# Own buffers and three move queues for the last two chunks, longer-counted stores, idle products up to the end

## The chip, the cores and the metric

The kernel runs on one core of one Trainium2 chip. The metric is the device time of one execution in microseconds; the median of the runs is given. Profiles are of one execution, with times from the first instruction of the span. Five engines work side by side, each in its own order: TensorE (PE; PEld is its weight loads), VectorE (DVE), ScalarE (ACT), GpSimd (POOL) and SyncE (SP); SP, ACT and POOL also issue DMAs.

## What is computed

A linear recurrence with a state per head, and behind it a gated projection with a causal convolution. All is float32; `B, H, S, D = 4, 8, 768, 40`.

```python
state = zeros(B, H, D, D)
for t in range(S):
    y[t]  = r[t] @ state                       # per head
    Sa    = state @ a[t]
    state = state * w[t] - outer(Sa, b[t]) + outer(v[t], k[t])

x = y as [B, S, 320]
gate = sigmoid(sum(conv_w[k] * x shifted by 4 - k  for k in range(5)))
out  = (gate * (x @ w_val)) @ w_out
```

## The kernel before

Time is cut into 12 chunks of 64 steps. For each chunk a preparation (`prep`, L458) makes cumulative decays with two scans on VectorE and scales the inputs; `tri` (L528) inverts triangular 32x32 blocks for two chunks at once in many small steps on VectorE; `solve` (L562) builds the 64x64 inverses on TensorE; `chain` (L614) is the recurrence itself. A chain works in two halves `hf` (8 of 16 head pairs each) through products `u0`, `u`, `t`, `g`, `ys`, each followed by an eviction on ACT or VectorE. Its last eviction `ye` (L680) writes the chunk's output x into `XE[c % 2]`.

Behind the chain stands the gated projection:

- `moves(c)` (L735) rearranges x for the projection by DMAs from `xe` to `xt`: 8 for the first half of the heads, 4 for the second (L742). For chunks 0 to 9 they go on POOL, for the last two, which `single` (L732) picks out, on SP.
- `moe(c)` (L746) runs once for each pair of chunks 0 to 9 (after the odd one), and once for each of chunks 10 and 11. Its steps, with names: `cv` (the convolution: one step of three pieces on ACT, L755, then four steps of three pieces on VectorE, L759), `gate` (sigmoid on ACT, L763), `val` (x @ w_val on TensorE, L89, in two parts), `gm` (gate times value on VectorE, L765 and L768), `out` (the product with w_out, L112), `os` (its eviction on ACT, L773), `store` (DMA to HBM, L780; on ACT, for chunk 11 every second one on SP). `val` and `out` use one pair of PSUM banks, PM, so they take turns with `gm` and `os`.
- `room(c)` (L724) says where this lies. Pairs use all of `XTW` (tile `xt`) for the input and `AG` (tile `ag`) for convolution, gate and product; the stored result is written over the convolution. Chunks 10 and 11 use a half each of the same two tiles, and so wait for the pair before them by the keys `XK`, `AK`, `GK`.

The order of the work is planned before the kernel is built. `Plan.op` (L155) registers each step with its engine, a duration in ns, what it reads and writes, and `lat`, the time from its end until another engine may use its result. `Plan.order` (L176) runs a greedy list scheduler with 80 random starts and 5 refinements each over all steps of the whole kernel, walks each order through a model of the engines, and keeps the one with the shortest modelled time. Each engine then executes its steps in exactly that order. Where the model sees TensorE waiting for over 0.48 us, `greedy` (L198) puts in idle products on a constant (L221 to L229, emitted at L832), which keep TensorE occupied; each goes to a PSUM bank that is free at that time.

`KB` (tile `kb`) is a ring of two tiles with the inputs k and b of a chunk; `prep`, `ak` (L494) and `turn` (L508) read it. The last of the 12 chunks' readers are done some 60 us before the last chunk's chain begins to write its output. `ind` is a constant operand of the scans; column C of it is overwritten by each chunk's `rc` (L469) and reset by `ic` (L473).

Of the kernel before, what the change touches and what calls it, by code (L numbers as in the profile page):

```python
# [147 lines left out]
class Plan:  # L148
# [27 lines left out]
    def order(self, fill):  # L176
# [21 lines left out]
        def greedy(rank, before, after, gap, tensor=None, weight=0, slack=0):  # L198
# [9 lines left out]
            for _ in range(N):  # L208
# [12 lines left out]
                if pe and end[cst]:  # L221
                    x = max(free["PE"], end[cst] + 3000)
                    while x + WARM + 150 < t:
                        k = next((k for k in banks if last[k] + 1 < len(users[k]) and eng[users[k][last[k] + 1]] == "PE" and
                                  (last[k] < 0 or eng[users[k][last[k]]] != "PE" and end[users[k][last[k]]] + 300 < x)), None)
                        if k is None:
                            break
                        more.append((x, -1 - banks.index(k)))
                        x = tensor.run(x, WARM, 4, 384)  # L229
# [103 lines left out]
def fast_path(ctx, tc, ins, out, nch, cst, wts, wz, wmx, fl):  # L333
# [37 lines left out]
    XE = ring("xe", 2, [128, P16, C + 4])  # L371
    XTW = new("xt", [128, 2 * 680])
    AG = new("ag", [128, 40 * C])
# [84 lines left out]
    def prep(c):  # L458
# [6 lines left out]
        def flat(x):  # L465
# [6 lines left out]
           r=wk + [("wpad", int(c == 1)), "ind"], w=["y0"])  # L472
        op(("ic", c), "DVE", 60, lambda: V.memset(ind[:, :, C:C + 1], WLO ** C), w=["ind"])  # L473
        op(("far", c), "ACT", act(1024) + 140, lambda: A.activation(out=wv, in_=wv, func=AF.Abs, bias=bias[:, 0:1]), r=["bias"], w=wk)
# [225 lines left out]
    def weigh():  # L700
# [3 lines left out]
        for i in range(NWT // WB):  # L704
            f = (XTW if i % 2 else AG)[:, 0:4 * WB].bitcast(I32)
            keys = XK if i % 2 else AK + GK[0:2]

            def wload(i=i, f=f):
                st_[i] = convert_ops(nc, f, wts[:, i * WB:(i + 1) * WB])
                dma(f[:, 0:2 * WB], src[:, 2 * i * WB:2 * (i + 1) * WB])  # L710
            op(("wd", i), "SP", 870, wload, w=keys, lat=2500)
            for j in range(8):
                op(("wc", i, j), "DVE", WCD[j], lambda i=i, j=j: st_[i][j](), w=keys + ["wts"])
# [7 lines left out]
    wv, wo, cw = weights(wts, wz)  # L721
    XK, AK, GK = [("xt", 0), ("xt", 1)], [("acc", 0), ("acc", 1)], [("gv", 0), ("gv", 1), "n1"]

    def room(c):  # L724

        i, L = c % 2, C if single(c) else 2 * C
        h = i if single(c) else 0
        xt = XTW[:, h * 680:h * 680 + 10 * (L + 4)].rearrange("p (b t) -> p b t", b=10)
        acc, gf = [AG[:, o + h * 640:o + h * 640 + 10 * L] for o in (0, 20 * C)]
        return (L, xt, acc, gf) + ((XK[i:i + 1], AK[i:i + 1], GK[i:i + 1]) if single(c) else (XK, AK, GK))  # L730

    def single(c):  # L732
        return c + 2 >= nch

    def moves(c):  # L735
# [3 lines left out]
        for hf in range(2):  # L739
            def xd(hf=hf):  # L740
                for o, x in x_moves(xt, XE[i], C, hf, lo, at):
                    (nc.sync if single(c) else G).dma_start(out=o, in_=x)  # L742
            op(("xd", c, hf), "SP" if single(c) else "POOL", (8, 4)[hf] * (400 if single(c) else 600), xd,
               r=[("xe", i, hf)] + ([] if lo else [("xe", i, "c")]) + ["wts"], w=xk, lat=2500)

    def moe(c):  # L746
# [5 lines left out]
        nn = [4 * L, 4 * L, 2 * L]  # L752
        part = [[("cv", x, k) for x in ((c % 2,) if single(c) else (0, 1))] for k in range(3)]
        for k, q in enumerate(qs):
# [19 lines left out]
        for b in range(B):  # L774
# [3 lines left out]
            else:  # L778
                to, of = out[b, c * C - C:c * C + C], accf[:, b * DM:b * DM + DM]
            op(("store", c, b), on, 560, lambda to=to, of=of, eng=eng: eng.dma_start(out=to, in_=of), r=ak, lat=2000)  # L780

# [187 lines left out]
```

## Time and profile before

| | before |
|---|---|
| median of 3 runs | 457.69 us (457.06 to 459.44) |
| profiled execution: its time / its span | 458.0 us / 456.2 us |
| mean granted TensorE clock | 0.961 of full |
| busy: TensorE / VectorE / ACT / POOL | 407.6 / 351.0 / 216.8 / 81.4 us |
| moved by DMA | 63.15 MB |

Busy time of TensorE contains the idle products, and its matmuls are pipelined, so a busy TensorE is not one at its peak. The granted clock is a share of full speed (2.4 GHz); half is 1.2 GHz.

### The profile page before, as it was taken

The numbers are of one execution on the slowest core, as the hardware profiler recorded it, in microseconds if no ns is written. First come the engines' busy times: TensorE is split into PE (matmuls) and PEld (weight loads), VectorE is DVE, ScalarE is ACT, GpSimd is POOL, SyncE is SP. The second block draws the span as 40 slices with busy tenths as digits, with TensorE's granted clock in tenths as the row PEclk, the third lists the DMA queues.
The fourth block names the chain that finished last, engine by engine and source line by source line (L and its number), as shares of the span: only waits on it lengthen the run. The fifth ranks groups of instructions, "written<-read, shape, count | busy, mean of one in ns | idle before, by whom it ended". The sixth has DMA issues, their size and how long they took to land.

```text
span 456.2 us, 19899 instructions
## 1 busy us (share of the span) xinstructions
PE 407.6 (89%) x9007; PEld 346.5 (76%) x9007; DVE 351.0 (77%) x673; ACT 216.8 (48%) x368; POOL 81.4 (18%) x169
## 2 busy tenths in 40 slices
PE   0799989899999899989999599989999999999773
PEld 0798868888988688888877588877797787778551
DVE  8999968999988959889899389949898950823530
ACT  1963466364962452973706490804772355333110
POOL 2010000236000515000461000007600533000000
PEclk9999999999999999999999799979999999999956
DMA  8897320575605525624665304533304235002111
GB/s 330 337 356 251 101 105 4 178 244 189 222 4 170 188 73 191 225 57 164 225 207 153 136 5 168 208 123 116 90 4 168 57 120 178 3 18 74 31 30 34
DMA packets 19689, 63.15 MB, mean 138 GB/s; under 512 B 4576, under 2 KB 8944, under 8 KB 16528
## 3 DMA queue, kind: packets, MB, share of 16 engines
q1 hardware_dynamic: 12400, 54.64, 34.4%
q0 software_dynamic: 3840, 3.42, 3.0%
q10 hardware_dynamic: 3360, 3.77, 2.5%
q8 instruction: 72, 1.18, 1.1%
q14 instruction: 17, 0.14, 0.1%
HBM read 53.77 MB, written 3.93 MB: 126 GB/s over the span
## 4 chain that ended last, share of the span: by engine, by line
PE 77%; ACT 7%; issue 4%; DMA 3%; SPq 2%; DVE 1%; ACTq 0%; DVEq 0%
PE pc L653 9%; PE pm L89 9%; PE pc L667 8%; PE pm L112 8%; PE pp L502 5%; PE pm L832 5%; PE pp L514 4%; PE pc L643 4%; PE pc L669 4%; PE pc L627 3%; DMA out<-ag 3%; PE pc L636 3%; PE pc L625 2%; PE pp L484 2%; PE pc L832 2%
## 5 line engine op out<-in xcount | busy, mean ns | idle before, releaser
L742 POOL DMA_DIRECT2D xt<-xe x120 | 73.8, 622 | 193.7 <-PE pm L89 100.4
L759 DVE SCALAR_TENSOR_TENSOR ag<-xt,wts,ag 128x512 f32<-128x512 f32 (+2 forms) x84 | 47.4, 590 | 13.5 <-ACT ag L755 9.7
L655 DVE TENSOR_TENSOR mu<-pc,cst 128x1024 f32<-128x1024 f32 x24 | 29.3, 1222 | 35.9 <-PE pc L653 28.1
L554 DVE TENSOR_TENSOR tm<-x 128x58 f32<-128x58 f32 (+9 forms) x164 | 51.9, 317 | 2.8
L556 DVE TENSOR_TENSOR x<-x,tm 128x58 f32<-128x58 f32 (+9 forms) x164 | 52.0, 317 | 2.3
L653 PE MATMUL pc<-ra,vu 64*128 64x64 f32 x768 | 47.2, 277 | 3.1 <-issue 2.8
L653 PEld LDWEIGHTS pc<-ra,vu 64*128 64x128 f32 x768 | 45.0, 191 | 4.6 <-issue 2.9
L832 PE MATMUL pm<-cst 128*128 128x192 f32 x218 | 42.5, 343 | 2.1 <-ACT tt L590 1.6
L667 PE MATMUL pc<-mu,kbt 128*64 128x104 f32 x768 | 40.7, 261 | 0.0
L112 PE MATMUL pm<-wts,ag 128*128 128x320 f32 (+1 forms) x144 | 39.8, 473 | 0.8 <-DVE ag L768 0.8
L832 PEld LDWEIGHTS pm<-cst 128*128 128x128 f32 x218 | 36.3, 196 | 3.7 <-ACT tt L590 2.1
L667 PEld LDWEIGHTS pc<-mu,kbt 128*64 128x64 f32 x768 | 36.0, 140 | 3.1 <-issue 0.2
L89 PE MATMUL pm<-xt,wts 128*128 128x256 f32 (+3 forms) x168 | 33.4, 383 | 4.6 <-ACT ag L773 2.9
L112 PEld LDWEIGHTS pm<-wts,ag 128*128 128x128 f32 (+1 forms) x144 | 22.0, 196 | 14.0 <-issue 6.9
L516 ACT COPY kbt<-pp 128x640 f32<-128x640 f32 x24 | 16.6, 693 | 32.1 <-PE pp L514 16.8
L89 PEld LDWEIGHTS pm<-xt,wts 128*128 128x128 f32 (+1 forms) x168 | 23.4, 189 | 10.9 <-ACT ag L773 3.4
L478 DVE TENSOR_TENSOR kb<-kb,y 104x1024 f32<-104x1024 f32 x24 | 29.0, 1212 | 1.0 <-DMA kb<-in_kb 0.9
L484 PE MATMUL pp<-at,kb 64*64 64x64 f32 x768 | 15.5, 234 | 16.0 <-DVE kb L478 13.3
L688 ACT COPY zd<-pc 104x320 f32<-104x320 f32 x22 | 9.1, 428 | 42.7 <-PE pc L685 25.4
L484 PEld LDWEIGHTS pp<-at,kb 64*64 64x64 f32 x768 | 13.7, 146 | 18.5 <-DVE kb L478 13.6
L502 PE MATMUL pp<-at,kb 64*64 64x64 f32 x768 | 25.5, 220 | 1.6 <-issue 1.1
L502 PEld LDWEIGHTS pp<-at,kb 64*64 64x64 f32 x768 | 23.6, 135 | 4.1 <-issue 1.7
(110 smaller groups left out, 757.6 us busy)
## 6 DMA issues: line engine op xcount, KB each, us to landing
kb<-in_kb SPq DMA_DIRECT2D x12, 1024.0 KB
vu<-in_vt SPq DMA_DIRECT2D x12, 1024.0 KB
ra<-in_ra SPq DMA_DIRECT2D x12, 832.0 KB
at<-in_a SPq DMA_DIRECT2D x12, 512.0 KB
w<-in_w SPq DMA_DIRECT2D x11, 520.0 KB
vp<-in_vp SPq DMA_DIRECT2D x12, 320.0 KB
out<-ag ACTq DMA_DIRECT2D x20, 160.0 KB
xt<-xe POOLq DMA_DIRECT2D x30, 42.5 KB, 3.7
```

The costliest lines, as they stand in the source:

```text
L89: T.matmul(out=o, lhsT=wv[k][r, m * 128:min(m * 128 + 128, DM)], rhs=rhs, start=(k == 0), stop=(k == 2))
L112: nc.tensor.matmul(out=ps[:, j, 0:DM], lhsT=gv[r, q:q + 128], rhs=wo[k][r], start=(k == 0), stop=(k == 2))
L484: T.matmul(out=PP[rows(par ^ s, 64), s, q * C:q * C + C], lhsT=KB[kb][rk, 2 * q + s, 1], rhs=at[rk, 2 * q + s], start=True, stop=True)
L502: T.matmul(out=PP[r, s, q * C:q * C + C], lhsT=KB[kb][r, 2 * q + s, 0], rhs=AT[n][r, 2 * q + s], start=True, stop=True)
L554: V.tensor_tensor(out=tv, in0=part(32 * (j + 1) + j, *b, (32, n), (0, j)), in1=part(32 * j, *b, (0, n), (1, j)), op=ALU.mult)
L556: V.tensor_tensor(out=x, in0=x, in1=tv, op=ALU.subtract)
L653: T.matmul(out=ps[:, s, i * C:i * C + C], lhsT=vu[r, 8 * hf + i].rearrange("p b t -> p (b t)"), rhs=ra[r, w, 0:C], start=True, stop=True)
L655: op(("ge", c, hf), "DVE", dve(1024), lambda: V.tensor_tensor(out=mu[:, :, 0:C].rearrange("p (i s) t -> p s i t", s=2), in0=ps.rearrange(" ...
L667: T.matmul(out=o, lhsT=KBT[k][:, y * D:y * D + C], rhs=mu[:, 2 * (4 * p + q4) + s], start=(not c and not q4), stop=(q4 == 3))
L742: (nc.sync if single(c) else G).dma_start(out=o, in_=x)
L759: op(("cv", c, j, k), "DVE", 130 + 1.04 * nn[k], lambda k=k, q=q, j=j: V.scalar_tensor_tensor(out=acc[:, q], in0=xt[:, q, j:j + L], scalar ...
L832: return lambda: T.matmul(out=bank[:, 1, 0:192], lhsT=ident, rhs=cst[:, 0:192], start=True, stop=True)
```

## The change

1. Idle products may also go to a bank that has no user left, not only to one whose next user is TensorE.
2. `XTW` shrinks to what a pair needs. Chunks 10 and 11 take input, convolution and product from `KB[0]` and `KB[1]`, with keys of their own; the keys of pairs become single names.
3. `moves`: a table of queues with a planned cost for each issue (SP 750, POOL 550, ACT 600 ns), and `split`, which deals out the DMAs of each half: for pairs all on POOL as before (planned at 550 instead of 600 ns), for chunk 10 on SP (4 and 2) and POOL (4 and 2), for chunk 11 on SP (3 and 1), POOL (3 and 2) and ACT (2 and 1). Each share is a step of its own in the plan.
4. The latency that the plan counts for a store is 6000 instead of 2000 ns.
5. The reset `ic` of `ind` becomes a copy on ACT from the column beside it, instead of a memset on VectorE.

```diff
-                        k = next((k for k in banks if last[k] + 1 < len(users[k]) and eng[users[k][last[k] + 1]] == "PE" and
+                        k = next((k for k in banks if (last[k] + 1 == len(users[k]) or eng[users[k][last[k] + 1]] == "PE") and
                                   (last[k] < 0 or eng[users[k][last[k]]] != "PE" and end[users[k][last[k]]] + 300 < x)), None)
...
-    XTW = new("xt", [128, 2 * 680])
+    XTW = new("xt", [128, 10 * (2 * C + 4)])
...
-        op(("ic", c), "DVE", 60, lambda: V.memset(ind[:, :, C:C + 1], WLO ** C), w=["ind"])
+        op(("ic", c), "ACT", 150, lambda: A.copy(out=ind[:, :, C], in_=ind[:, :, C - 1]), w=["ind"])
...
-            keys = XK if i % 2 else AK + GK[0:2]
+            keys = XK if i % 2 else AK + GK[0:1]
...
-    XK, AK, GK = [("xt", 0), ("xt", 1)], [("acc", 0), ("acc", 1)], [("gv", 0), ("gv", 1), "n1"]
-
-    def room(c):
-
-        i, L = c % 2, C if single(c) else 2 * C
-        h = i if single(c) else 0
-        xt = XTW[:, h * 680:h * 680 + 10 * (L + 4)].rearrange("p (b t) -> p b t", b=10)
-        acc, gf = [AG[:, o + h * 640:o + h * 640 + 10 * L] for o in (0, 20 * C)]
-        return (L, xt, acc, gf) + ((XK[i:i + 1], AK[i:i + 1], GK[i:i + 1]) if single(c) else (XK, AK, GK))
+    XK, AK, GK = ["xt"], ["acc"], ["gv", "n1"]
+
+    QUEUES = {"SP": (nc.sync, 750), "POOL": (G, 550), "ACT": (A, 600)}
 
     def single(c):
         return c + 2 >= nch
+
+    def split(c):
+
+        if not single(c):
+            return {"POOL": (8, 4)}
+        return {"SP": (3, 1), "POOL": (3, 2), "ACT": (2, 1)} if c + 1 == nch else {"SP": (4, 2), "POOL": (4, 2)}
+
+    def room(c):
+
+        if not single(c):
+            return 2 * C, XTW[:, 0:10 * (2 * C + 4)].rearrange("p (b t) -> p b t", b=10), AG[:, 0:20 * C], AG[:, 20 * C:40 * C], XK, AK, GK
+        x = KB[c % 2].rearrange("p u s t -> p (u s t)")
+        keys = [("xt", c, hf, on) for hf in range(2) for on in split(c)]
+        return C, x[:, 0:680].rearrange("p (b t) -> p b t", b=10), x[:, 680:1320], x[:, 1320:1960], keys, [("acc", c)], [("gv", c)]
...
         for hf in range(2):
-            def xd(hf=hf):
-                for o, x in x_moves(xt, XE[i], C, hf, lo, at):
-                    (nc.sync if single(c) else G).dma_start(out=o, in_=x)
-            op(("xd", c, hf), "SP" if single(c) else "POOL", (8, 4)[hf] * (400 if single(c) else 600), xd,
-               r=[("xe", i, hf)] + ([] if lo else [("xe", i, "c")]) + ["wts"], w=xk, lat=2500)
+            todo = list(x_moves(xt, XE[i], C, hf, lo, at))
+            for on, n in split(c).items():
+                eng, each = QUEUES[on]
+                now, todo = todo[:n[hf]], todo[n[hf]:]
+
+                def xd(now=now, eng=eng):
+                    for o, x in now:
+                        eng.dma_start(out=o, in_=x)
+                op(("xd", c, hf, on), on, each * n[hf], xd, r=[("xe", i, hf)] + ([] if lo else [("xe", i, "c")]) + ["wts"],
+                   w=[("xt", c, hf, on)] if single(c) else xk, lat=2500)
...
-        part = [[("cv", x, k) for x in ((c % 2,) if single(c) else (0, 1))] for k in range(3)]
+        part = [[("cv", c if single(c) else -1, k)] for k in range(3)]
...
-            op(("store", c, b), on, 560, lambda to=to, of=of, eng=eng: eng.dma_start(out=to, in_=of), r=ak, lat=2000)
+            op(("store", c, b), on, 560, lambda to=to, of=of, eng=eng: eng.dma_start(out=to, in_=of), r=ak, lat=6000)
```

## Rows read from the trace of the kernel before

**Rows 1.** The page, 40 equal slices of the span: granted clock in tenths of full.

```profile
PEclk9999999999999999999999799979999999999956
```

**Rows 2.** By stretches: us, their length, then each engine's busy us, clock, DMA share, GB/s.

```profile
175.00:234.30 59.30, 58.06 (x1458) 50.31 (x1456) 53.51 (x92) 34.07 (x58) 16.95 (x33) 1.00 0.52 172
234.30:308.20 73.90, 64.76 (x1454) 55.72 (x1450) 55.72 (x104) 34.59 (x59) 6.65 (x16) 0.91 0.40 135
...
379.60:424.70 45.10, 44.41 (x973) 36.34 (x960) 20.57 (x36) 17.60 (x36) 2.56 (x4) 1.00 0.15 50
424.70:456.20 31.50, 18.93 (x90) 12.33 (x88) 7.37 (x19) 4.05 (x7) 0.00 (x0) 0.71 0.13 34
...
432.30:435.10 2.80, 0.00 (x0) 0.00 (x0) 1.97 (x6) 1.41 (x4) 0.00 (x0) 0.90 0.09 31
435.10:443.60 8.50, 7.28 (x36) 5.58 (x36) 3.39 (x9) 0.74 (x1) 0.00 (x0) 0.50 0.17 39
```

**Rows 3.** The chain that ended last, its end: start us, us, what.

```profile
423.34 0.72 SPq L742
...
431.92 1.99 DMA xt<-xe
...
434.40 0.68 ACT ag L773
...
449.13 0.69 ACT ag L773
```

**Rows 4.** VectorE in time at the end: start us, us, what, [idle before <-releaser].

```profile
422.59 0.68 DVE L680 TENSOR_TENSOR xe<-pc,lam 104x512 f32<-104x512 f32 x1
...
423.98 0.68 DVE L680 TENSOR_TENSOR xe<-pc,lam 104x512 f32<-104x512 f32 x1
...
426.90 0.69 DVE L765 TENSOR_TENSOR ag<-pm,ag 128x512 f32<-128x512 f32 x1 [1.20 <-PE pm L89]
428.72 0.29 DVE L768 TENSOR_TENSOR ag<-pm,ag 128x128 f32<-128x128 f32 x1 [1.13 <-PE pm L89]
...
440.79 0.69 DVE L765 TENSOR_TENSOR ag<-pm,ag 128x512 f32<-128x512 f32 x1 [3.27 <-PE pm L89]
443.32 0.29 DVE L768 TENSOR_TENSOR ag<-pm,ag 128x128 f32<-128x128 f32 x1 [1.84 <-PE pm L89]
```

**Rows 5.** TensorE in time at the end, columns as in rows 4.

```profile
423.70 1.16 PE L89 MATMUL pm<-xt,wts 128*128 128x128 f32 x8
...
429.07 3.16 PE L112 MATMUL pm<-wts,ag 128*128 128x320 f32 x12 [0.40 <-DVE ag L768]
435.13 2.08 PE L89 MATMUL pm<-xt,wts 128*128 128x128 f32 x8 [2.90 <-ACT ag L773]
...
443.67 5.37 PE L112 MATMUL pm<-wts,ag 128*128 128x320 f32 x12 [0.40 <-DVE ag L768]
```

**Rows 6.** Around 250 us: the chain, ACT in time, three stretches as in rows 2.

```profile
248.42 8.31 DMA out<-ag
...
256.84 0.72 ACT L755 ACTIVATE ag<-xt,wts 128x512 f32<-128x512 f32 x1 [5.84 <-DMA out<-ag]
...
249.90:254.40 4.50, 4.41 (x26) 4.11 (x26) 0.20 (x1) 1.04 (x1) 0.00 (x0) 1.00 0.96 358
254.40:259.00 4.60, 0.00 (x0) 0.00 (x0) 1.41 (x3) 2.11 (x3) 0.00 (x0) 0.79 0.12 44
259.00:265.00 6.00, 5.94 (x170) 5.33 (x172) 5.16 (x11) 5.81 (x12) 0.74 (x6) 0.59 0.01 3
```

**Rows 7.** Line L742, the moves: duration ns min/median/max, first and last start, and landing.

```profile
L742 POOL DMA_DIRECT2D xt<-xe x120: 554/646/794, 88.1 to 382.5; - x120
...
DMA to landing us min/median/max: 1.7/3.3/7.1
```

**Rows 8.** Idle products, costliest groups of the page: busy us, mean ns of one.

```profile
L832 PE MATMUL pm<-cst 128*128 128x192 f32 x218 | 42.5, 343 | 2.1 <-ACT tt L590 1.6
```

**Rows 9.** The reset of `ind` on VectorE, and a small copy on ACT, columns as before.

```profile
L473 DVE MEMSET ind<- x12: 72/72/72, 11.4 to 320.8; 104x16 f32 x12
...
175.69 0.24 ACT L697 COPY xe<-xe 104x64 f32<-104x64 f32 x1 [8.68 <-DVE xe L680]
```

## The prediction

> **What bounds the kernel now.** I read the granted clock by slices first. It is full nearly everywhere and falls in two places: at slices 23 and 27, and in the last two slices [rows 1]. Then I read the busy times by stretches. Between the last evictions of chunks 5 and 7, 73.9 us pass; the pair before took 59.3 us for the same work, so one stretch holds some 14 us that another does without. From 379.6 us to 424.7 us TensorE is the bound: 44.41 us busy of 45.10, at full clock, with VectorE at 20.57 [rows 2]. After that the picture turns over: 31.5 us of span in which TensorE idles for a whole stretch (432.3 to 435.1 us) and then works at 0.50 of its clock, the lower of its two levels (1.2 and 2.4 GHz) [rows 2].
>
> The end is therefore a chain of its own, and the chain of waits tells it. Chunk 11's second half of state output leaves VectorE at 424.66 us (423.98 plus 0.68) [rows 4]; call that moment T. Its twelve moves into `xt` are issued on SP one behind the other, from 423.34 us until 431.88 us, and the last lands 1.99 us after its issue, at 433.91 us [rows 3]. Meanwhile TensorE ends chunk 10's output product at 432.23 us (429.07 plus 3.16), but its eviction `os` starts only at 434.40 us: it stands on ACT behind chunk 11's first convolution steps, which wait for those moves [rows 3, 5]. Chunk 11's `val` needs the bank that `os` empties; it starts at 435.13 us at half clock. From `val` to the eviction at 449.13 us nothing else runs; stores and closing take the last 7.07 us of the span [rows 3, 5].
>
> The stretch from 234.3 us holds the other place. At 248.42 us the chain passes into 8.31 us of waiting for stores of `ag`; ACT stands 5.84 us in front of the next pair's convolution. The engines of the DMA are 0.96 busy then, since loads run beside the stores. TensorE is busy with idle products at first, then with nothing (0.00 of 4.60 us), and comes back at a clock of 0.79 to 0.59 [rows 6].
>
> **The end, part by part.** The profiled execution took 458.0 us for a span of 456.2 us; the median of the runs is 457.69 us, 0.3 us less. The sum is made against 458.0.
>
> *Own buffers.* Chunks 10 and 11 get their input, convolution and gated product in the two `kb` tiles, which have had their last reader by then. So chunk 10's convolution no longer waits for the stores of chunks 8 and 9. Nothing is added but names; the cost is zero, covered by the fact that no load goes to `kb` any more.
>
> *Moves on three queues.* Of chunk 11's 8 and 4 moves SP keeps 3 and 1, POOL gets 3 and 2, ACT 2 and 1. POOL is the slowest: 0.646 us an issue, 3.3 us to landing [rows 7]. Its first three go from 423.27 us (the first half's eviction, 422.59 plus 0.68 [rows 4]) to 425.2 us, its last two to 426.5 us, landing at 429.8 us instead of 433.91. Queued behind them on POOL is nothing. On ACT the three issues stand before what ACT does next, so a late eviction of chunk 11 would hold chunk 10's `os`, but by T both halves are out. By POOL's longest landing (7.1 us [rows 7]) the data would be there at 433.6 us. Then `val` of chunk 11 would start 0.6 us later than I put it below; I take zero, the median's value.
>
> *The eviction set free.* With the data there at 429.8 us ACT has its convolution steps done before 432.23 us, and `os` can start 0.09 us behind the product, as it does for chunk 11 (449.04 to 449.13 us) [rows 3, 5]. That is worth 434.40 - 432.32 = 2.1 us.
>
> *Idle products to the end.* The old rule lets an idle product go only to a bank whose next user is TensorE; the new one also to banks with no user left, and the `pp` banks have none in the end. Where the plan sees TensorE waiting, the gap is filled. At full clock chunk 10's pieces show the prices. `val` to the first gating took 3.20 us (423.70 to 426.90) against 5.66 us (435.13 to 440.79) for chunk 11; the second `val` 1.13 against 1.84 us of VectorE's waiting; the output product 3.16 against 5.37 us [rows 4, 5]. Saved: 2.46 + 0.71 + 2.21 = 5.4 us. The gate must not come later than the first gating: the last convolution steps would be done about 3 us after 429.8 us, ahead of 436.2 us. Each idle product is 0.343 us long [rows 8] and TensorE works in order, so on average half of one stands before real work: 0.17 us at each of five waits, 0.9 us lost (0 to 1.7).
>
> Sum of the end: 2.1 + 5.4 - 0.9 = 6.6 us gained. Its bounds: 2.1 us if the clock falls all the same, and 9.3 us if TensorE had only its work from 423.70 us on (chunk 10 took 8.5 us from 423.70 to 432.23 us, 1.0 us of it two gatings, so 7.5 us of work; two chunks of that, one chunk's gatings of 1.0 us that nothing covers, and 0.8 us of eviction end at 440.5 instead of 449.82 us).
>
> **The rest.** *Stores counted at 6 us instead of 2.* The plan now keeps the next convolution 6 us behind its stores, and puts other work on ACT and VectorE there. What was missed at 248 us is 8.31 us, so 2.3 us of waiting may stay, and 5.84 - 2.3 = 3.5 us go [rows 6]. Bounds: 0, if other work is just as late, and 5.84. I take 3.5, since the row of the wait itself is the nearest there is. The Trainium skill ("DMA: Bandwidth & Descriptors", section "Anatomy of one DMA — SWDGE (gpsimd) path") gives a DMA about 2.0 us and its bytes at 436 GB/s, which for a 160 KB store is, as an estimate, 2.4 us. By that the old count was right, this term is 0, and the time would be 451.1 us; the 8.31 us of [rows 6] disagree, so I keep 3.5.
>
> *The reset of `ind` from VectorE to ACT.* Twelve memsets of 0.072 us leave VectorE (0.9 us), twelve small copies enter ACT, 0.24 us as its nearest row [rows 9], 2.9 us spread over an engine that is 34 us busy in a pair of 59 to 74 us [rows 2]. The next scan now waits for ACT; only where the scans follow one another, in the first 40 us, could that be felt. Between -0.9 and +2.9 us; I take 0.
>
> *A new order.* Costs, names and waits of the plan change, so its search draws another order for the whole kernel. I take zero for that, the middle between a stretch like the shortest pair and one like the longest [rows 2], and give it room in the range.
>
> Sum: 458.0 - 6.6 - 3.5 = 447.9 us, or **447.6 us** beside the median.
>
> **The rivals.** *The waiting for stores is not regained* (or comes up at another pair): only the end is gained, 458.0 - 6.6 - 0.3 = 451.1 us. For it: the DMA share was 0.96 whatever the count said; against it: the wait is the one thing that the new count addresses. Chance 0.22.
>
> *The clock falls anyway.* Real waits longer than planned (POOL's landing against the 2.5 us of the plan) leave TensorE idle before `val`; it was 2.9 us of idling at 432.2 us that went before the half clock [rows 2, 5]. Then the end gives 2.1 us: 458.0 - 2.1 - 3.5 - 0.3 = 452.1 us. Against it: the gap itself shrinks to an eviction. Chance 0.10.
>
> *One more hole.* The new order meets one stall like that of 249.9 us at another pair: TensorE is without real work from 249.9 to 259.0 us, 9.1 us, while the old one goes: 458.0 - 6.6 - 3.5 + 9.1 - 0.3 = 456.7 us, no change to be measured. Chance 0.08.
>
> *Slower.* The hole of 249.9 us stays and a second one opens at another pair, because ACT, in order, stands before a store that loads hold up. Its price is 9.1 us and the half-speed stretch behind it (5.94 us of TensorE at 0.59, 2.4 us too long [rows 6]), 11.5 us: 458.0 - 6.6 + 11.5 - 0.3 = 462.6 us. It decides from 6.6 + 2.3 = 8.9 us on. For it: the pairs differ by 14.6 us already [rows 2]. Chance 0.10.
>
> **How the numbers follow.** The forecast has 0.50. A measurement of this kernel can tell about 0.5%, 2.3 us, from no change. Faster is the forecast and the first two rivals, 0.82; the same 0.08; slower 0.10. The low end takes the best of both terms, 458.0 - 9.3 - 5.8 - 0.3 = 442.6, and a little for the order: 442.0. The high end holds the clock's rival with 3 us of order added: 455.0. Outside lie the last two rivals, 0.18.
>
> **What would show it.** Right: the clock full in the last stretch up to the last product; `os` of chunk 10 within 0.2 us of its product; from T to the last eviction's start 18 us instead of 24.5; no ACT wait over 3 us for stores. Wrong: chunk 11's `val` still at 0.50, moves landing later than 9 us behind T, idle products ahead of ready work, or T itself beyond 424.7 us: that would be the order, and the end's gain would be given back there.

## The result, and the profile after

The changed kernel took 460.53 us (median of 20 runs, one of which took 956.54 us, unexplained) beside 456.49 us for the kernel before (20 runs taken in turn with them). The ratio is 1.0109, with an interval of 1.0067 to 1.0151: **slower by 1.1%**, where 447.6 us and faster were forecast. The ratios here leave out runs more than 1.5% above the fastest of their own kernel, and both kernels scatter by more than that, so the medians of all runs stand beside them in the table below, where the profiled runs of e2_redraw_after, e5, e11, f1 and f2 are such runs.

The profiled run of the changed kernel took 458.48 us with a span of 456.6 us, almost that of before (458.0 and 456.2 us). Its granted clock in 40 slices:

```profile
PEclk9999989989979999979999999999999999599999
```

The last two slices are now full, where [rows 1] ended in 5 and 6. But there is a new 5 at slice 35, and small dips at four places before it. The stretches between the last evictions of state output (line L680), columns as in [rows 2]:

```profile
175.11:247.94 72.83, 66.32 (x1482) 56.83 (x1480) 60.38 (x118) 35.20 (x62) 15.85 (x32) 0.95 0.43 142
247.94:308.08 60.14, 56.43 (x1449) 48.79 (x1446) 54.01 (x95) 34.57 (x60) 14.11 (x28) 1.00 0.52 171
...
378.13:410.63 32.50, 30.23 (x696) 25.31 (x695) 13.83 (x23) 12.50 (x27) 8.50 (x14) 0.79 0.14 44
410.63:434.93 24.30, 24.30 (x469) 19.61 (x470) 9.43 (x19) 7.43 (x15) 3.21 (x7) 1.00 0.14 45
```

The slow pair has changed places: chunks 3 to 5 now take 72.8 us and chunks 5 to 7 60.1 us, where [rows 2] have 59.3 and 73.9. The last two rows are new. From chunk 9's eviction to chunk 10's it is 32.5 us, and to chunk 11's another 24.3 us. Before, the same two stretches were:

```profile
379.59:402.21 22.62, 21.93 (x528) 18.26 (x514) 12.54 (x20) 10.53 (x22) 2.56 (x4) 1.00 0.16 52
402.21:423.98 21.77, 21.77 (x443) 17.41 (x443) 7.32 (x16) 7.07 (x14) 0.00 (x0) 1.00 0.15 49
```

So T, the end of chunk 11's second state output, lies at 435.62 us (434.93 plus 0.69) instead of 424.66: 11.0 us later, 9.9 of them from chunk 9 to chunk 10. The end of the kernel after, VectorE, TensorE and ACT in time, columns as in [rows 4]:

```profile
434.93 0.69 DVE L680 TENSOR_TENSOR xe<-pc,lam 104x512 f32<-104x512 f32 x1 [1.76 <-PE pc L667]
...
436.08 3.16 PE L112 MATMUL pm<-wts,kb 128*128 128x320 f32 x12 [0.39 <-DVE kb L781]
439.17 0.92 PE L845 MATMUL pp<-cst 128*128 128x192 f32 x4
440.08 1.16 PE L89 MATMUL pm<-kb,wts 128*128 128x128 f32 x8
...
447.76 3.16 PE L112 MATMUL pm<-wts,kb 128*128 128x320 f32 x12 [0.39 <-DVE kb L781]
...
439.33 0.69 ACT L786 COPY kb<-pm 128x640 f32<-128x640 f32 x1 [14.35 <-PE pm L112]
439.92 0.40 ACT L768 ACTIVATE kb<-kb,wts 128x128 f32<-128x128 f32 x1
...
451.01 0.69 ACT L786 COPY kb<-pm 128x640 f32<-128x640 f32 x1 [5.44 <-PE pm L112]
```

From T to the start of the last eviction (L786) it is 451.01 - 435.62 = 15.4 us; [rows 3, 4] have 449.13 - 424.66 = 24.5. `val` and the output product of chunk 11 run at their full-clock lengths (1.16 and 3.16 us, as chunk 10's in [rows 5]); chunk 10's eviction starts 0.1 us behind its product. It can, since the new order puts it ahead of chunk 11's first convolution steps on ACT (439.33 us, they start at 439.92); before, it stood behind them. The moves into the own buffer, with T at 435.62:

```profile
L755 POOL DMA_DIRECT2D kb<-xe x5: 505/514/529, 433.7 to 436.4; - x5
...
DMA to landing us min/median/max: 1.6/1.8/2.0
```

The last of these five is issued at 436.4 us and lands 2.0 us later at most, 2.8 us behind T, where I had put 5.1. The balance of the two profiled runs is: T 11.0 us later, the end 9.1 us shorter, the time from the last eviction's start to the end of the span 1.5 us shorter (7.07 to 5.6 us); together +0.4 us, the difference of the two spans. The end did more than I forecast, and what lies before T gave it back. Some of both is only moved: chunk 10's first `val` products, which e1_order below has mostly behind T, stand ahead of T here. The shorter time behind the last eviction was not in my sum. It goes with the new buffers in most runs: the six profiled kernels that store chunk 11 from `ag` take 7.0 to 7.2 us there, nine of the twelve that store from `kb` 5.5 to 5.7, and three 6.5 to 7.5 (e7, e10, f4); why wasn't followed.

### The profile page after: what moved, and what is told of

Read it like the earlier page. It is cut to its first block, busy times and chain, and to the rows that moved or that the text cites. A ratio compares the mean times of both kernels' runs of the same rounds, so it can differ in the third digit from the quotient of the medians.

```text
span 456.6 us, 19925 instructions
## 1 busy us (share of the span) xinstructions
PE 408.2 (89%) x9023; PEld 351.1 (77%) x9023; DVE 351.6 (77%) x661; ACT 217.9 (48%) x380; POOL 87.5 (19%) x180
## 4 chain that ended last, share of the span: by engine, by line
PE 71%; ACT 8%; DMA 8%; issue 4%; DVE 3%; POOL 0%; ACTq 0%; DVEq 0%
PE pc L653 10%; PE pm L89 9%; PE pc L667 8%; PE pm L112 8%; PE pp L502 5%; PE pc L669 4%; PE pc L643 4%; DMA out<-ag 4%; PE pp L514 4%; PE pc L636 3%; PE pc L627 3%; DMA xt<-xe 2%; PE pc L625 2%; PE pc L685 2%; PE pm L579 2%
## 5 line engine op out<-in xcount | busy, mean ns | idle before, releaser
L772 DVE SCALAR_TENSOR_TENSOR ag<-xt,wts,ag 128x512 f32<-128x512 f32 (+1 forms) x60 | 38.6, 654 | 24.0 <-ACT ag L768 23.9
L845 PE MATMUL pm<-cst 128*128 128x192 f32 x242 | 47.5, 348 | 2.1 <-ACT tt L590 1.6
L845 PEld LDWEIGHTS pm<-cst 128*128 128x128 f32 x242 | 41.4, 200 | 4.0 <-ACT tt L590 2.4
L667 PEld LDWEIGHTS pc<-mu,kbt 128*64 128x64 f32 x768 | 34.7, 137 | 3.0
L502 PE MATMUL pp<-at,kb 64*64 64x64 f32 x768 | 28.2, 235 | 6.9 <-ACT mb L492 6.8
L502 PEld LDWEIGHTS pp<-at,kb 64*64 64x64 f32 x768 | 26.4, 149 | 8.9 <-ACT mb L492 7.8
L112 PE MATMUL pm<-wts,ag 128*128 128x320 f32 (+1 forms) x120 | 31.2, 454 | 0.0
L484 PE MATMUL pp<-at,kb 64*64 64x64 f32 x768 | 15.5, 229 | 15.5 <-DVE kb L478 13.7
L89 PE MATMUL pm<-xt,wts 128*128 128x256 f32 (+1 forms) x120 | 27.3, 410 | 0.0
L484 PEld LDWEIGHTS pp<-at,kb 64*64 64x64 f32 x768 | 13.6, 142 | 17.6 <-DVE kb L478 14.0
L541 POOL MEMSET x<- 128x256 f32 (+4 forms) x30 | 4.0, 186 | 114.2 <-DVE x L533 114.2
L514 PE MATMUL pp<-cst,kb 104*128 104x104 f32 x192 | 22.0, 257 | 4.1 <-issue 3.4
```

Source lines behind the costliest of these rows:

```text
L89: T.matmul(out=o, lhsT=wv[k][r, m * 128:min(m * 128 + 128, DM)], rhs=rhs, start=(k == 0), stop=(k == 2))
L112: nc.tensor.matmul(out=ps[:, j, 0:DM], lhsT=gv[r, q:q + 128], rhs=wo[k][r], start=(k == 0), stop=(k == 2))
L502: T.matmul(out=PP[r, s, q * C:q * C + C], lhsT=KB[kb][r, 2 * q + s, 0], rhs=AT[n][r, 2 * q + s], start=True, stop=True)
L514: T.transpose(out=PP[:, i // 4, i % 4 * 128:i % 4 * 128 + ER], in_=KB[kb][0:ER, 8 * x + i].rearrange("p b t -> p (b t)"), identity=ident[0 ...
L667: T.matmul(out=o, lhsT=KBT[k][:, y * D:y * D + C], rhs=mu[:, 2 * (4 * p + q4) + s], start=(not c and not q4), stop=(q4 == 3))
L772: op(("cv", c, j, k), "DVE", 130 + 1.04 * nn[k], lambda k=k, q=q, j=j: V.scalar_tensor_tensor(out=acc[:, q], in0=xt[:, q, j:j + L], scalar ...
```

## The experiments

Two theories at first. **The order**: the parts gain what was forecast at the end, and the redrawn order of the whole kernel loses it before T. **A part**: one of the parts itself costs time before T (the reset on ACT, the new count of the stores, the larger `xt`), whatever the order. All kernels, with the kernel before in the same session; T and the end (T to the last eviction's start) are from the profiled run:

| run | what it is | median us (runs) | before us | ratio, interval | T | end |
|---|---|---|---|---|---|---|
| e1_order | the change in the old order | 447.48 (6) | 454.89 | 0.992, 0.984-1.000 | 421.3 | 17.1 |
| e2_redraw_before | before, another draw | 460.38 (6) | 454.89 | 1.020, 1.007-1.032 | 425.9 | 23.0 |
| e2_redraw_after | the change, another draw | 459.77 (6) | 454.89 | 1.011, 0.995-1.027 | 438.6 | 15.6 |
| e3_fill | the change, 11 more idle products | 458.83 (6) | 454.89 | 1.016, 1.005-1.027 | 438.6 | 15.4 |
| e4_lat_only | before, stores counted at 6 us | 454.95 (12) | 456.15 | 1.009, 0.999-1.019 | 420.5 | 20.6 |
| e5_lat2000 | the change, stores at 2 us | 463.52 (6) | 456.15 | 1.012, 1.004-1.019 | 443.0 | 15.4 |
| e6_nofill | e1 without idle products at the end | 451.45 (6) | 456.15 | 0.989, 0.982-0.996 | 422.8 | 17.1 |
| e8_fill_before | before, idle products at the end | 453.05 (12) | 456.15 | 0.996, 0.992-1.000 | 421.0 | 19.4 |
| e7_sp | e1, last moves all on SP | 455.15 (6) | 458.71 | 0.990, 0.976-1.004 | 425.2 | 18.8 |
| e9_draw_before | before, a third draw | 456.47 (12) | 458.71 | 0.995, 0.990-1.000 | 428.4 | 19.4 |
| e10_draw_after | the change, a third draw | 464.74 (6) | 458.71 | 1.011, 0.997-1.024 | 435.9 | 16.9 |
| e11_reset_dve | the change, reset on VectorE | 455.14 (12) | 458.71 | 0.988, 0.983-0.994 | 433.7 | 15.6 |
| f1_late10 | the change, chunk 10's `val` late | 454.76 (12) | 456.62 | 0.998, 0.993-1.003 | 431.5 | 21.0 |
| f2_old_fill | the change, old rule of the fills | 467.62 (6) | 456.62 | 1.022, 1.013-1.030 | 442.8 | 18.1 |
| f3_reset_act | before, reset on ACT | 471.00 (6) | 456.62 | none | 437.2 | 21.6 |
| f4_hole | e1, work moved ahead of the store wait | 450.78 (6) | 456.62 | 0.987, 0.981-0.994 | 426.2 | 17.1 |

### The parts without the new order

e1_order has all of the change, but its steps stand in the order of the kernel before, as a written list; only the projection, the moves and the last convolutions of chunks 10 and 11 are placed anew:

```diff
-    seq = plan.order({...})
+    seq = plan.given({...})   # emits the steps of the list ORDER, and its idle products
```

> All parts of the change, but everything outside the projection of chunks 10 and 11 (and its moves) stands in the order that the kernel before had; only these steps are placed anew among it. Theory 'order': the parts gain at the end what the changed kernel shows there (15.4 us from the last eviction of chunk 11 to the last `os`, against 24.5 us before), and the redrawn order gave it back around 385 us (TensorE at 0.50 of its clock from 388 to 400 us). So here 7 to 9 us faster than before, chunk 11's last eviction within 2 us of 424.7 us, clock full at 385 to 400 us. Rival 'parts': a part itself costs in the middle (the reset on ACT, chunk 10's products earlier on TensorE); then chunk 11's last eviction is 6 to 11 us late here too, and the time within 1% of before.

It took 447.48 us beside 454.89: **7.4 us less by the medians**. All six runs (444.5 to 449.3 us) lie below all but one of the eleven of before, and two kernels that keep this order but for a few steps (e6, f4) are 4.7 and 5.8 us below the kernel before of their sessions. That it meets the 447.6 us of my forecast is luck: I had forecast 10.1 us less, 3.5 of them from the stores, which did not come, and the kernel before, run in turn with it, was itself 2.8 us faster than its 457.69. Its clock in slices, and its two stretches in front of T:

```profile
PEclk9999999999999999999999969998999999999999
```

```profile
376.16:399.05 22.89, 21.94 (x528) 18.26 (x514) 12.54 (x21) 10.53 (x22) 4.67 (x8) 1.00 0.18 60
399.05:420.65 21.60, 21.60 (x442) 17.23 (x442) 9.27 (x18) 7.54 (x15) 2.22 (x5) 1.00 0.14 44
```

They are as long as those of before (22.6 and 21.8 us), at full clock, with as many products. The resets on ACT lie ahead of them, the last at 319.2 us; T, which has everything before it, is 421.3 us, where three runs of the old order have 420.5 to 424.7 (e4, e8, before). So no cost of the parts before T shows when the order is the old one.

Is a new draw enough to lose some us? In e2_redraw_before and e2_redraw_after nothing is changed but the start of the search's random numbers:

```diff
-            rnd = random.Random(seed)
+            rnd = random.Random(seed + 1000)
```

> The kernel before, with nothing changed but the start numbers of the 80 random orders that its plan searches (1000 to 1079 instead of 0 to 79). Theory 'order': a mere redraw moves the time by as much as the change did, 3 to 10 us either way. Rival 'parts': the search ends in orders of equal worth, so within 2 us of before.

> The changed kernel with the start numbers of its random orders moved by 1000, nothing else. Theory 'order': the end keeps its 15 to 17 us and the place where chunk 11's last eviction falls moves by several us; the time is anywhere from 8 us faster to 5 us slower than the kernel before. Rival 'parts': chunk 11's last eviction is at 433 to 437 us again and the time 1% above before.

The kernel before, drawn again, took 5.5 us more by the medians. Its profiled run, 457.8 us, has T at 425.9 us, near before's, so it doesn't show where the medians' loss lies. The change, drawn again, has T at 438.6 us, as late as the first time. So a draw is worth several us, as the first theory wants, but the late T seems to belong to the change's draws and not to chance alone. I come back to that below.

### What the late T is made of

The stretch from 378 to 411 us of the kernel after, in slices of 2 us and in the chain of waits:

```profile
380.00:382.00 2.00, 2.00 (x106) 1.75 (x97) 0.00 (x0) 1.39 (x5) 2.00 (x4) 1.00 0.30 85
382.00:384.00 2.00, 1.59 (x58) 1.22 (x57) 0.40 (x2) 1.23 (x5) 2.00 (x5) 1.00 0.13 29
384.00:386.00 2.00, 1.41 (x107) 1.25 (x100) 0.00 (x0) 0.99 (x2) 2.00 (x4) 1.00 0.35 58
386.00:388.00 2.00, 1.04 (x46) 0.91 (x45) 0.00 (x0) 0.59 (x2) 0.49 (x1) 0.89 0.66 206
388.00:390.00 2.00, 2.00 (x40) 1.72 (x40) 0.00 (x0) 1.38 (x4) 0.00 (x0) 0.50 0.03 8
...
398.00:400.00 2.00, 2.00 (x6) 1.17 (x7) 1.97 (x4) 0.00 (x0) 0.00 (x0) 0.50 0.00 0
```

```profile
385.41 1.55 issue
...
392.27 3.61 PE pc L653 x32
395.88 7.67 PE pm L89 x24
```

From 380 to 388 us TensorE has little but short products, of `solve` (L596, L604) and of the next chain's `u0` and `u`, and is busy 6.0 of 8 us, 1.55 us of the rest in a wait of its own ("issue"). Then it stands at 0.50, the lower level, from 388 to 400 us, while it works without a pause: `val` of the pair (8, 9) takes 7.67 us. e3_fill keeps this order, step for step, and puts 11 idle products between the short ones from 380 to 392 us.

> The changed kernel in its own order, with eleven idle products of 0.33 us put between TensorE's short products of chunks 10 and 11 at 380 to 392 us, where it was busy 6.0 of 8 us and the clock fell to 0.50 until 401 us. If the fallen clock is what this stretch lost: clock full there, chunk 9's first `val` 5.1 instead of 7.7 us, chunk 11's last eviction 3 to 6 us earlier, the time 3 to 6 us under the changed kernel's (0.7 to 1.3%). Rival: the stretch waits for ACT and VectorE and the idle products only add up to 3.6 us; then the same or up to 3.6 us slower than the changed kernel.

```profile
385.06:413.56 28.50, 27.93 (x718) 23.73 (x717) 13.83 (x24) 12.51 (x27) 8.49 (x14) 1.00 0.16 49
```

The clock stays at 1.00 and the stretch is 28.5 instead of 32.5 us. TensorE's own wait is gone in e3 too. It stood within these products of `solve`, first in the kernel after, then in e3:

```profile
386.96 0.32 PE L596 MATMUL pm<-dd,mb 32*32 32x32 f32 x14 [1.55 <-issue]
...
393.04 0.75 PE L656 MATMUL pm<-dd,mb 32*32 32x32 f32 x64
```

They end 9.2 us behind chunk 9's eviction in the one and 8.7 in the other, since idle products took the time that the wait had taken. So **some 3.6 of the 4.0 us were the clock**. e5_lat2000 and f2_old_fill, further down, have this order without e3's idle products: 31.0 and 31.8 us, with the same wait (1.82 and 1.55 us) and then 10 and 14 us at half clock.

What lets the clock fall, the short products or that wait, is not separated. In e10, e11 and f3 too it falls in this stretch, for 10 us or more, within 2 us of such a wait of 1.3 to 2.0 us; in e9 a wait of 1.84 us passes at full clock. Nor does the late T need the clock: e2_redraw_after takes 32.1 us here at 1.00.

```profile
380.41:412.52 32.11, 30.71 (x736) 25.52 (x734) 19.32 (x36) 16.27 (x34) 7.30 (x14) 1.00 0.21 63
```

The other 5.6 us of e3 beside e1's 22.9 are more to do. The new order puts 696 products into this stretch and the old one 528: 102 more of `solve` and 64 more of `u0`, with waits between them that the idle products now fill. Up to chunk 11's eviction there are another 27 and 2.7 us, since chunk 10's `val` stands ahead of it. For that, chunk 9's eviction comes no sooner than in e1 (378.13 us beside 376.16): some time was lost ahead of it as well, and where wasn't followed. In the total, 458.83 us, the 4.0 us can't be told: in its profiled run the clock fell in other places instead.

### The count of the stores

e4_lat_only is the kernel before with the new count, e5_lat2000 the change with the old one:

```diff
-            op(("store", c, b), on, 560, ..., r=ak, lat=2000)
+            op(("store", c, b), on, 560, ..., r=ak, lat=6000)
```

> The kernel before with one part of the change alone: stores counted at 6000 instead of 2000 ns, so the plan draws a new order. Theory 'count': the longer count drives the search to worse orders in the middle; then chunk 11's last eviction moves from 425 us to 433 us or later, as in both orders drawn for the changed kernel (435.6 and 438.6 us), and the time is 8 us or more above before. Rival 'any redraw': this is one more draw like that with other start numbers (5.5 us above before, eviction at 425.9 us); 0 to 6 us above before. In both ACT's waits for stores, 9.2 us before, show what the count is worth: under 4 us if my term for it was right, 9 us or more if not.

> The changed kernel with one part undone: stores counted at 2000 ns again; the plan draws a new order. Theory 'count': the middle comes back, chunk 11's last eviction at 424 to 428 us, the end keeps its 15 to 17 us, the time 5 to 9 us under before. Rival 'any redraw': the eviction stays at 430 us or later and the time within 1% of before or above.

Neither changed the order of a single step: on every engine e4's instructions stand as before's, and e5's as the changed kernel's. So the count is worth **nothing**, and the two are repeats: they show by how much one order scatters. T is 420.5 us in e4 and was 424.66, and the end 20.6 us where it was 24.5, since the clock fell later in it; e5 has T at 443.0 us for 435.6, the end at 15.4 us in both. The medians are 454.95 beside before's 456.15, and 463.52 us. Since e4 is before's own order, its median of 1.2 us less and its ratio of 1.009 suggest that in so few runs neither tells a difference under 1%. ACT's waits for the stores in before and after (in all, times, the longest, us):

```profile
ACT ag L755 <- DMA out<-ag: 9.2, 3, 5.8
```

```profile
ACT ag L768 <- DMA out<-ag: 9.2, 3, 5.9
```

The long one only moved, from 256.8 to 196.0 us, with the slow pair. In e4 these waits are 10.2 us, in e5 9.6. f4_hole asks what it is worth to have other work there: in e1's list two convolution steps of chunk 5 on ACT and two on VectorE, at 250 us, are put behind seven and four other steps of these engines, and 9 idle products there are left out.

```diff
-... cv(5,0,1) cv(5,0,0) cv(5,1,1) cv(5,2,1) ... 7 on ACT, 4 on DVE ... cv(5,3,1) ...
+... 7 on ACT, 4 on DVE ... cv(5,0,1) cv(5,0,0) cv(5,1,1) cv(5,2,1) cv(5,3,1) ...
```

> The kernel e1_order, with one place of its order changed by hand: around 250 us two convolution steps on ACT and the two on VectorE that follow them stand behind seven other steps of ACT and four of VectorE, so that nothing stands behind the wait for the stores, and nine of the thirteen idle products in front of the next product are left out. If that wait is worth what it lasts: ACT's wait for stores under 1 us there instead of 5.6, the hole in TensorE's work (9 us) down to 2 or 3, and 3 to 6 us less than e1_order. If other work is just as late, as my lower bound had it: the wait goes and the time stays within 1.5 us of e1_order.

ACT's wait falls from 5.6 us in e1 to 1.3, but the chain goes on through the stores:

```profile
ACT ag L828 <- DMA out<-ag: 1.3, 1, 1.3
```

```profile
249.64 0.34 ACTq L853
249.97 0.04 issue
250.01 9.03 DMA out<-ag
```

The stretch from chunk 5 to chunk 7 is 69.9 us instead of e1's 71.6, and the total, 450.78 us, is not below e1's. But f4 does not show that the wait is worth nothing. Behind the stores its clock stands at 0.50 for 17 us, e1's for 7, and one step of the chain alone, at half and at full clock, takes 3.3 us more, first f4, then e1:

```profile
268.86 7.02 PE pc L713 x64
...
270.48 3.72 PE pc L713 x64
```

Whether the nine idle products left out did that wasn't tested. For a store of 160 KB the Trainium skill ("DMA: Bandwidth & Descriptors", section "Anatomy of one DMA — SWDGE (gpsimd) path") gave an estimate of 2.4 us; the 9.03 us disagree, as [rows 6] did. That section is on DMAs that GpSimd issues, and these stores are issued on ACT. The rival that had the estimate for it was right in that the waiting was not regained, but for another reason: the plan did not change.

### Idle products, buffers and queues at the end

e8_fill_before is the kernel before, in its own order, with 10 idle products ahead of chunk 11's two `val` products and nothing else. e6_nofill is e1 without its 6 at the end. f2_old_fill is the changed kernel with the old rule; its steps stand as in the changed kernel, and 11 idle products at the end are gone.

```diff
-                        k = next((k for k in banks if (last[k] + 1 == len(users[k]) or eng[...] == "PE") and
+                        k = next((k for k in banks if last[k] + 1 < len(users[k]) and eng[...] == "PE" and
```

> The kernel before, in its own order, with ten idle products added at its end and nothing else: eight in front of chunk 11's first `val`, where TensorE stood idle for 2.9 us, and two in front of its second. If the idle before `val` is what lets the clock fall: clock full from there, 5.4 us less from `val` to the last eviction, the end 19 us instead of 24.5 and the time 4 to 5.4 us under before. If the products of chunk 10 before it were too thin already, the clock falls all the same and the time stays within 1 us.

> The kernel e1_order, less the six idle products that stand in its end. Theory 'gap': what kept the clock up at the end is that TensorE no longer stands idle for 2.9 us before chunk 11's `val`, since the gaps left are under 1 us; then the clock stays full and the time within 1 us of e1_order (447.5 us). Rival 'idle products', the step of the prediction: without them the clock falls to half before chunk 11's products, the end grows from 17.1 to some 22 us, the time is 4 to 5.4 us above e1_order.

> The changed kernel with the old rule for idle products. All steps stand in the same order as in the changed kernel; eleven idle products of the end are gone. If they carry the end, as the prediction had it: the clock falls at the end, from chunk 11's last eviction to the last `os` 19 to 21 us instead of 15.4, the time 4 to 5 us above the changed kernel's. If the moves' earlier landing carries it: the end within 1 us of 15.4, the time within 1.5 us of the changed kernel's.

In e8 the clock is full to the last product and the end is 19.4 us: 5.1 us less than in the profiled run of before, for my 5.4, but 1.2 us less than in e4, the same order in a run whose clock fell later. The total is 3.1 us less by the medians. In e6, with buffers and queues, the clock stays full without them, with waits of 0.8 us ahead of the products, and the end is 17.1 us in e1 and e6. In f2 it does fall. Its TensorE and its clock near the end:

```profile
453.50 1.12 PE L89 MATMUL pm<-kb,wts 128*64 128x128 f32 x8 [3.17 <-DVE kb L778]
454.56 0.69 PE L89 MATMUL pm<-kb,wz 64*64 64x128 f32 x4
455.64 5.12 PE L112 MATMUL pm<-wts,kb 128*128 128x320 f32 x12 [0.39 <-DVE kb L781]
```

```profile
455.00:460.00 5.00, 4.61 (x14) 2.57 (x10) 0.29 (x1) 0.00 (x0) 0.00 (x0) 0.54 0.02 7
```

TensorE waits 3.17 us for the gating, then the output product takes 5.12 us for 3.16. So buffers with queues, and idle products, are two remedies for the same idling. The first alone is enough where it leaves short gaps (e1's order), and not where it leaves 3 us. With buffers and queues in place the idle products add between 0 (e6) and 2.7 us (f2) to the end's gain. By medians e6 is 4.0 us above e1 in different sessions, 2.7 less the sessions' difference, and f2 is 7.1 us above the changed kernel and 4.1 above e5, which has the same order: not settled.

e7_sp is e1 with all twelve moves of each of the last two chunks on SP:

```diff
-        return {"SP": (3, 1), "POOL": (3, 2), "ACT": (2, 1)} if c + 1 == nch else {"SP": (4, 2), "POOL": (4, 2)}
+        return {"SP": (8, 4)}
```

> The kernel e1_order with one part undone: all moves of chunks 10 and 11 on SP, one behind the other, at their old places in the order; buffers, idle products and everything else stay. By the prediction's step the moves' issue sets when chunk 11's `val` can start: the twelve end 9 us behind the first half's eviction and land 2 us later, 6 us behind the data of e1_order, so `val`, which waits 8.4 us behind chunk 11's last eviction there anyway, starts some 1 to 2 us later, and so does the last eviction: 447.5 plus 1 to 3 us. Rival: `os` of chunk 10, which stands on ACT behind chunk 11's convolution steps, is held too and the clock falls in the gap; then 5 us or more above e1_order.

```profile
422.80 0.72 SPq L815
...
430.35 0.71 SPq L815
431.05 0.04 issue
431.10 2.00 DMA kb<-xe
...
433.98 0.67 ACT L846 COPY kb<-pm 128x640 f32<-128x640 f32 x1
...
443.97 0.69 ACT kb L846
```

The chain again runs over SP's issues and one landing, as in [rows 3], and the end is 18.8 us for 17.1: the three queues are worth **1.7 us** in the profiled runs. By medians, each beside the kernel before of its session, e7 gains 3.6 us and e1 7.4. Chunk 10's eviction (433.98 us) starts 1.1 us behind its product here, again behind chunk 11's first convolution steps. So in this order it is the queues that set it free, and not the buffers; e7, with the buffers and one queue, is only 0.6 us below e8, which has idle products in the old ones (19.4 us).

### Where the bad orders come from

Two more draws, by the same edit with 2000 for 1000; the change with the reset left on VectorE; the reset on ACT alone in the kernel before; and the change with chunk 10's first `val` made to wait for chunk 11's evictions, which puts it about where the old order has it.

```diff
-        op(("ic", c), "ACT", 150, lambda: A.copy(out=ind[:, :, C], in_=ind[:, :, C - 1]), w=["ind"])
+        op(("ic", c), "DVE", 60, lambda: V.memset(ind[:, :, C:C + 1], WLO ** C), w=["ind"])
```

That is e11_reset_dve; f3_reset_act is the reverse in the kernel before. In f1_late10 (`moe(10)` is also listed after chunk 11's chain and moves):

```diff
-        op(("val", c, 0), "PE", ..., r=xk + ["wts", "wz"], w=pmb, ...)
+        op(("val", c, 0), "PE", ..., r=xk + ["wts", "wz"] + ([("xe", 1, 0), ("xe", 1, 1)] if c == 10 else []), w=pmb, ...)
```

> The kernel before with the start numbers of its random orders moved by 2000: a third draw of the same work. Theory 'any redraw': as far from before as the second draw was, 0 to 8 us above, chunk 11's last eviction between 420 and 430 us. Rival 'the parts push': the draws of the unchanged steps stay near before (within 3 us on the whole), only those of the changed steps are worse.

> The changed kernel with its start numbers moved by 2000: a third draw. Theory 'any redraw': its middle is as good as one drawn for the unchanged steps as often as not; chunk 11's last eviction anywhere from 420 to 440 us, the time from 445 to 465 us. Rival 'the parts push': the eviction at 432 us or later for the third time and the time over 456 us, since the search now may put chunk 10's projection and the work before it in places where TensorE's work gets thin and its clock falls.

> The changed kernel with one part undone: the reset of `ind` stays a memset on VectorE; the plan draws a new order. If the copies on ACT are what made the orders of the changed kernel bad: chunk 11's last eviction at 420 to 428 us and the time 445 to 451 us. If not: like the other draws of the changed kernel, eviction at 432 us or later, 456 us or more.

> The changed kernel, but chunk 10's first `val` may not start before chunk 11's last evictions, as was the case in the kernel before; the plan draws a new order. Theory 'freedom': the early placing of chunk 10's projection is what spoils TensorE's stretch before the end; then chunk 11's last eviction is back at 420 to 428 us, the end 17 to 19 us, the time 3 to 8 us under before. Rival 'any redraw': the eviction between 425 and 440 us, less the 3 us of products that now follow it, and the time within 1% of before.

> The kernel before with one part alone: the reset of `ind` as a copy on ACT; the plan draws a new order. If this part pushes the search to bad orders: 5 us or more above before, chunk 11's last eviction beyond 430 us with the old end of 20 to 25 us. If not: one more draw of the unchanged steps, within 5 us of before, the eviction at 420 to 429 us.

Three draws of the kernel before have T at 424.7, 425.9 and 428.4 us; three of the change at 435.6, 438.6 and 435.9. Repeats of the two first orders widen this to 420.5 and to 443.0 us (e4, e5), and still the two groups lie 7 us apart. So does the stretch from chunk 9's to chunk 11's last eviction: 44.4, 47.8 and 48.3 us in the draws of before, 56.8, 57.5 and 53.8 in those of the change. With the reset on VectorE the change's T is 433.7 us, this stretch 53.9, and the total 3.6 us below before's. The reset on ACT alone puts T at 437.2 us, the stretch at 53.1, and the total at 471 us, 14.4 above before's. With the late `val` the stretch is 44.6 us, at full clock, as in the kernel before. T is 431.5 us all the same, since chunk 9's eviction comes late (386.2 us, in a run 5.2 us above the kernel's median); the late `val` also lengthens the end, to 21.0 us, and the total is 1.9 us below before's. The stretch in f1, in its two parts:

```profile
386.18:406.50 20.32, 19.11 (x600) 17.19 (x594) 12.09 (x21) 11.63 (x25) 3.35 (x6) 1.00 0.19 61
406.50:430.82 24.32, 23.93 (x454) 18.78 (x453) 9.87 (x19) 6.98 (x15) 3.51 (x8) 1.00 0.07 19
```

So the long stretch comes without the reset on ACT (e11), it comes without the new buffers and queues (f3), and it goes when chunk 10's `val` is late (f1). No single part makes it, and the reset's new engine drew the worst order (f3) without being the whole cause. It isn't the copies themselves: e1 has them too, and gains. Why the search ends in worse orders stays **open**. Each of these is a single draw, and draws of one kernel differ by several us (the two new draws of before lie 2.2 us below and 5.5 above the first in their sessions), so the 3.6 and the 1.9 us are no prices of the two edits; only f3's 14 us stand clear of that.

## Why the prediction was wrong, by its own steps

*What bounds the kernel.* Right: the end is a chain of its own, and each thing named in it (SP's issues, the eviction behind the convolution, the half clock) could be taken away with the effect on that chain.

*The end, 6.6 us.* The mechanism was right in the main, and so was the size: 9.1 us in the changed kernel and 7.4 in e1's order against the profiled run of before, 5.2 and 3.5 against e4's, whose clock fell later; 7.4 us by e1's medians, where the whole kernel counts. In e1's order the moves' earlier landing set the eviction free, as forecast; in the changed kernel it was the new order, which puts it ahead of chunk 11's convolution on ACT. POOL's moves landed 2.8 us behind T and not 5.1: their landing was 2.0 us at most with a quiet DMA, where I took the median of the whole kernel, 3.3 [rows 7], and I added it to the end of the issue, though that view counts from its start. The 0.9 us for idle products ahead of work did not show: the end is 17.1 us with them (e1) and without (e6). And 2.1 and 5.4 us are not two terms as I added them: e6 shows that the first can bring the second with it, f2 that it need not.

*Stores counted at 6 us, 3.5 us.* Failed: 0. I took for granted that another count changes the plan; e4 and e5 show that it changes no step. What the wait itself is worth stays open: with work put there by hand (f4) it shrinks by 4.3 us and the stretch by 1.7, but with 10 us more at half clock.

*The reset to ACT, 0.* Right for the copies in a given order (e1). Wrong for the one draw that they bring by themselves (f3).

*A new order, 0.* **This is the step that failed.** I took the middle between a good pair and a bad one and gave it 3 us of room. The scatter was there to be seen: two pairs of the same work differ by 14.6 us in [rows 2]. A draw costs several us by itself (e2), and the change's draws put T some 11 us later, against an end shorter by about 9. In the profiled run 9.9 of the 11.0 us lie between chunk 9's and chunk 10's last evictions, some 4 of them the half clock and the rest steps that the new order puts there. That T beyond 424.7 us would mean the order and give the end's gain back was named as the sign of being wrong, and it is what came.

*The rivals.* "Slower" had the sign right, 462.6 us for 460.5, by luck, since its mechanism was another: no second store hole opened (9.2 us of such waiting in both kernels); the loss is a stretch of short products with waits between them, the half clock behind it, and steps that stood ahead of chunk 9's eviction and now stand behind it. "One more hole", 456.7 us, is nearer to that in kind. "The clock falls anyway" did not come at the end. It came at 388 us, where I had no rival for it. The chances went wrong because I priced an order that is drawn by a search from what it is meant to do.

## What to carry to other kernels

Where a search draws the order of a kernel, every edit of a cost, a wait or an engine draws the whole order anew. Price that from the scatter between like stretches and not at zero, and separate it: put the edit into the old order, moving only the steps that it touches; here that is the version to keep (447.5 us). Two remedies for one idle gap don't add up: ask for each what is left when the other is in. A planner's count is worth something only if it changes a decision.

## What the runs showed of the hardware that was not expected

The same kernel scatters by 4%, and with the clock: the kernel before, in one session of 23 runs, ran from 446.55 us at a mean granted clock of 0.988 to 463.9 us; in another, from 447.45 us at 0.985 to 464.49 us at 0.944. The programs are the same; the places where the clock falls differ from run to run. Three runs, as I had them at first, don't show this (457.06 to 459.44 us).

TensorE lost its clock behind a stretch of short products in which it was busy 6.0 of 8 us, with a wait of its own of 1.55 us in it: 0.50 for 12 us. The same order with idle products between them had no such wait and kept 1.00 (e3). In the three profiled runs of this order without them, and in three other orders, the clock fell within 2 us of a wait of this kind.

A store that is issued beside loads took 8.3 and 9.0 us to be waited out [rows 6, f4's chain], while moves with a quiet DMA landed in 1.6 to 2.0 us, so a count for a DMA in a plan needs its neighbours and not only its size.
